# Hash-bucket attention and a MoE layer on one core: when output banks are evicted, who issues the stores, and three smaller edits

## The chip, the cores and the metric

One Trainium2 chip, one of its cores. The metric is device time in microseconds (us) of one execution. Engines: TensorE (PE, with PEld for its weight loads), VectorE (DVE), ScalarE (ACT), GpSimd (POOL) and SyncE (SP, which in this kernel issues DMAs).

## What is computed

Attention over 4 batches, 8 heads, 768 positions and 64 dimensions, where a query sees only the keys of its own hash bucket; then a two-layer feed-forward net, all to float32 accuracy.

```python
q_bits = einsum('bhsd,dk->bhsk', q, proj) > 0        # k has its own; proj is 64 x 6
mask = q_bucket[:, :, :, None] == k_bucket[:, :, None, :]
scores = where(mask, q @ k.T / 8, -1e9)
attn = softmax(scores) @ v
x = attn as [3072 tokens, 512]
h = x @ w_in                                         # 512 x 2048
g = where(h > 0, h, exp(min(h, 0)) - 1)
out = g @ w_out                                      # 2048 x 512
```

## The kernel before

Each float32 operand is scaled by a power of two and split into a float16 high half and a float16 low half; a product is then three float16 matmuls. `scaled` (L139 to L147, most of it ACT at L143) makes a high half, `rest` (L149 to L155, DVE at L152) a low half. The table `ENGINES` says which engine makes which half; its first entry holds while weights are still being decoded (`now[0]` is 0), its second after that.

The work goes in **slots**. A slot is one tile of scores: 128 queries of one head against all 768 keys (`scores`, L503): four matmuls into the one buffer of PSUM tile `s`, which DVE empties with a clamp that also takes the row maximum (`pt`, L519). Every second slot ACT takes the exponentials (L535), ACT and DVE split them into halves (`hl`), and SP transposes those by DMA (`PT`, L550). Six slots make a pair of heads for half a sequence, 24 a **chunk** (3 x 128 tokens); there are eight chunks, two to a batch. Four slots after a pair, `attend` multiplies with V (`av`, L558).

While slots of later chunks run, `moe_stream` gives PE the MoE of an earlier chunk in small pieces: for each of 16 blocks `f` of the hidden layer, `first` (12 matmuls into `h`, L584, then ACT at L595 and L598, DVE at L599, and the two halves of `g`), and two blocks later `second` (9 matmuls, L620: three for each of the chunk's three token tiles `t`). The results stay in PSUM for all 16 blocks: `banks` are two banks of one tile `o` (t = 0 and 1) and a tile `o2` (t = 2). At the last block each is evicted by `scaled("out", ...)` into one of two pieces of SBUF, `area["ot"]` (shown as `W`, for it lies in the tile of the weights), and stored to `out` (L632, by SP). ACT evicts t = 0 and 2, DVE t = 1 (L145). From slot 30 on the order on PE is the order in which the program was written (`manual_schedule`, L888); on the other engines, and before that slot, a scheduler places instructions.

In the first 40 slots or so the kernel also reads both weight matrices, which come as 64-bit numbers, decodes them to float32 (`wdecode`) and splits them (`wsplit`, 32 of them); `weights` (L833) hands this out, six steps a slot. For each batch V is loaded, its squares summed by ACT, and `scale` then takes the bound: a maximum over four sums (`vx`, DVE, L411), a matmul with ones that adds over the partitions (`sum`, PE, L184) and a few small DVE operations (`powers`); `vdue` (L774 to L779) says at which slot each of these steps is written. `behind_max` places DVE work behind the latest `pt`. K and Q of later pairs are prepared in the same way; their high halves are `n_hi`.

Of the kernel before, what the change touches and what calls it, by code (L numbers as in the profile page):

```python
# [10 lines left out]
F32 = mybir.dt.float32  # L11
I32 = mybir.dt.int32
AF = mybir.ActivationFunctionType
ALU = mybir.AluOpType
AX = mybir.AxisListType
# [32 lines left out]
ENGINES = {  # L48
    "p_hi": ("A", "A"),
    "p_lo": ("V", "V"),  # L50
    "n_hi": ("VA", "A"),
    "n_lo": ("V", "V"),
    "v_hi": ("A", "A"),
    "v_lo": ("V", "V"),
# [12 lines left out]
def lsh_attention_moe(  # L67
# [315 lines left out]
    def prep_v(b):  # L383
        st = {"f": [], "v": [None] * NP}

        def load():
            mx = small.tile([P, NP], F32, tag="vx", name="vx")
            for p in range(NP):
                f = vpool.tile([P, 2, NC, D], F32, tag="v", name="vf")
                with tc.issue_after(ks[b, V_AFTER]["done"].ins) if b == 0 else nullcontext():  # L390
                    nc.sync.dma_start(
                        f.rearrange("p h c d -> p h (c d)"),
                        v[b, 2 * p : 2 * p + 2].rearrange("h (p c) d -> p h (c d)", c=NC),
                    )
                st["f"].append(f)
            st["mx"] = mx
            if b == 0:
                for p in range(NP):
                    sums(p)

        def sums(p):
            f = st["f"][p]
            squares(st["mx"][:, p : p + 1], f.rearrange("p h c d -> p (h c d)"), steady.k1 if b else junk0)

        def scale():
            with behind_max():
                bound()

        def bound():
            m1 = small.tile([P, 1], F32, tag="vx1", name="vx1")  # L410
            nc.vector.tensor_reduce(m1, st["mx"], axis=AX.X, op=ALU.max)  # L411
            st["ex"], st["sc"] = powers(m1, 1, 2.0**-34, V_TOP, "v", squares=True)

        def split(p):
            f = st["f"][p]
            t = vpool.tile([P, 2, NC, 2, D], F16, tag="v", name="vhl")
            st["v"][p] = t
            for j in range(2):
                scaled("v_hi", t[:, j, :, 0, :], f[:, j], st["sc"])
                rest("v_lo", t[:, j, :, 1, :], f[:, j], st["sc"], t[:, j, :, 0, :])  # L420

        parts = [lambda p=p: sums(p) for p in range(NP)] if b else []
        return st, [load] + parts + [scale] + [lambda p=p: split(p) for p in range(NP)]


    wst = {}
# [142 lines left out]
        return x16  # L569


    def moe_stream(chunks):

        pend = []
        banks = []

        def first(c, f):
            w = c["nc"] * P
            h = ps_h.tile([P, 512], F32, tag="h", name="h")[:, :w]
            g, fc = f // FG, f % FG  # L580
            n = 0
            for t in range(KT):
                for wx, xx in ((0, 0), (0, 1), (1, 0)):
                    nc.tensor.matmul(  # L584
                        h,
                        WH[:, g * KT + t, wx, fc * P : (fc + 1) * P],
                        c["xs"][t][:, xx, :],
                        start=n == 0,
                        stop=n == 3 * KT - 1,
                    )  # L590
                    n += 1
                    if n < 3 * KT:
                        yield w
            e = part("e")[:, :w]
            nc.scalar.activation(e, h, AF.Exp, scale=c["ch"])  # L595

            hp = part("hp")[:, :w]
            nc.scalar.activation(hp, h, AF.Relu, scale=c["ch"])  # L598
            nc.vector.scalar_tensor_tensor(e, e, -1.0, hp, ALU.add, ALU.min)  # L599
            g16 = part("g").rearrange("p (x n) -> p x n", x=2)[:, :, :w]  # L600
            scaled("g_hi", g16[:, 0, :], e, c["sg"])
            rest("g_lo", g16[:, 1, :], e, c["sg"], g16[:, 0, :])
            pend.append((c, f, g16))
            yield w

        def second(c, f, g16):
# [11 lines left out]
            for t in range(n):  # L618
                for i, (gx, wx) in enumerate(((0, 0), (0, 1), (1, 0))):
# [4 lines left out]
                        start=f == 0 and i == 0,  # L624
                        stop=f == NF - 1 and i == 2,
                    )
                    if f == NF - 1 and i == 2:
                        rows = out[c["b"] * S : (c["b"] + 1) * S, :].rearrange("(p c) o -> p c o", c=NC)
                        ot = part("ot")
                        with tc.high_priority():  # L630
                            scaled("out", ot, o[t][:, :DO], c["os"])
                        nc.sync.dma_start(rows[:, c["c0"] + t, :], ot)  # L632
                    yield DO

        for c in chunks:
# [140 lines left out]
        vs[b] = prep_v(b)  # L776
    for b in range(1, B):
        s0 = [c for c in chunks if c["b"] < b][-1]["end"]
        vdue += [(s0 + x, s) for x, s in zip((-16, -14, -13, -12, -11, -9, -8, -2, 4, 10), vs[b][1])]  # L779


    wq = list(wsplits)
# [50 lines left out]
    def weights(n):  # L833
        nonlocal w_credit, w_at
        w_credit += n
        while w_credit >= 1:

            at = (w_at + (2 if w_at >= NSI else 1)) * SL
            users = {x[1] for x in due} | ({"v"} if len(vdue) == NP + 2 + (B - 1) * (2 * NP + 2) else set())
            if any(a < at + SL and at < z and users & u for a, z, u in guards):  # L840
                break
            if w_at not in w64 and w_at < NSI + NSO:
# [4 lines left out]
            elif w_at < NSI + NSO:  # L847
# [2 lines left out]
                load_w()  # L850
                if w_at in (NSI, NSI + NSO):
                    wscale(w_at // (NSI + NSO))
            elif wq:
                split_w()

    def turned(p, what):
        return p < 0 or what in ks[0, p]
# [94 lines left out]
```

## Time and profile before

| | |
|---|---|
| median of three runs | 966.19 us (963.73 to 966.58) |
| the profiled execution | 964.54 us, its span 962.7 us |
| PE busy | 825.0 us (86%) |
| ACT busy | 742.0 us (77%) |
| DVE busy | 705.7 us (73%) |
| POOL busy | 2.6 us |

The span goes from the first to the last instruction; the execution's own time is 1.84 us more. Busy shares are means over stages that differ: the first 175 us with the decoding of the weights, then attention and MoE together, then from about 890 us the MoE of the last chunk alone. What bounds a stage is read from its windows and waits.

### The profile page before, as it was taken

How to read it: one execution, taken by the hardware profiler on the slowest of the kernel's cores; microseconds unless marked ns; L12 is line 12 of the kernel's file. 1: busy time of each engine (PE TensorE's matmuls, PEld its weight loads, DVE VectorE, ACT ScalarE, POOL GpSimd, SP SyncE). 2: the span in 40 equal slices, each digit the busy share in tenths (PEclk: the TensorE clock that was granted, in tenths of full speed). 3: DMA queues.
4: the chain of work that ended last, by engine and by line, in shares of the span. 5: the costliest groups of instructions: out<-in, count | busy, mean ns of one | idle time of the engine just before them, and what ended most of it. 6: DMA issues, size and time to landing. Idle time of an engine off the chain costs nothing.

```text
span 962.7 us, 14525 instructions
## 1 busy us (share of the span) xinstructions
PE 825.0 (86%) x4975; PEld 422.4 (44%) x4975; DVE 705.7 (73%) x1528; ACT 742.0 (77%) x1469; POOL 2.6 (0%) x25
## 2 busy tenths in 40 slices
PE   2536555879989999889989998989989999999997
PEld 0113222434445555444545554544545454555453
DVE  6789899898877777678767686687877687665232
ACT  5667777999879787789779797698878788786443
POOL 1000000000000000000000000000000000000000
PEclk9998665999999999899999999999999999999999
DMA  9999988676886759486887666785786767656000
GB/s 284 264 201 215 223 213 179 131 151 139 158 177 151 151 107 144 97 186 120 166 188 135 127 130 122 136 165 102 143 168 126 125 116 149 100 99 99 33 1 33
DMA packets 406121, 138.46 MB, mean 144 GB/s; under 512 B 380960, under 2 KB 398880, under 8 KB 406048
## 3 DMA queue, kind: packets, MB, share of 16 engines
q1 hardware_dynamic: 405888, 137.54, 69.4%
q8 instruction: 39, 0.64, 0.3%
q14 instruction: 34, 0.28, 0.1%
q10 hardware_dynamic: 160, 0.00, 0.0%
HBM read 35.65 MB, written 6.29 MB: 44 GB/s over the span
## 4 chain that ended last, share of the span: by engine, by line
PE 55%; DVE 16%; DMA 15%; ACT 8%; issue 4%; SPq 1%; ACTq 0%; DVEq 0%
PE o L620 18%; PE h L584 18%; PE av L558 9%; PE s L507 7%; DVE pt L519 4%; DMA O<-nat1q 3%; DVE hl L152 3%; DMA K<-natk 3%; DMA PT<-hl 3%; ACT pt L535 3%; PE z L286 2%; ACT W L143 1%; DMA W<-in_moe_w_in_dram 1%; DVE U L152 1%; DVE natk L152 1%
## 5 line engine op out<-in xcount | busy, mean ns | idle before, releaser
L620 PE MATMUL o<-W,U 128*128 128x512 f16 x1152 | 283.8, 384 | 20.0 <-ACT W L143 20.0
L584 PE MATMUL h<-x,W 128*128 128x384 f16 x1536 | 284.1, 329 | 0.0
L584 PEld LDWEIGHTS <-W 128*128 128x128 f16 x1536 | 148.2, 98 | 123.8 <-issue 24.0
L519 DVE TENSOR_SCALAR_CACHE_REDUCE pt<-s 128x768 f32<-128x768 f32 x177 | 168.2, 950 | 42.8 <-PE s L507 41.6
L535 ACT ACTIVATE pt<-pt,nb,sg 128x768 f32<-128x768 f32 x192 | 195.3, 1019 | 1.8
L152 DVE SCALAR_TENSOR_TENSOR hl<-pt,r,hl 128x768 f16<-128x768 f32 x192 | 189.9, 1011 | 9.2 <-ACT hl L143 8.9
L143 ACT ACTIVATE hl<-pt,r 128x768 f16<-128x768 f32 x192 | 168.6, 926 | 32.7 <-DVE r L545 32.1
L620 PEld LDWEIGHTS <-U 128*128 128x128 f16 x1152 | 111.8, 98 | 141.6 <-issue 28.4
L507 PE MATMUL s<-K,O 128*128 128x384 f16 x708 | 152.7, 339 | 19.0 <-DVE pt L519 15.1
L558 PE MATMUL av<-PT,vhl 128*64 128x384 f16 x1152 | 114.9, 353 | 26.4 <-DMA PT<-hl 13.7
L599 DVE SCALAR_TENSOR_TENSOR U<-U 128x384 f32<-128x384 f32 x128 | 70.8, 553 | 79.5 <-ACT U L598 79.2
L507 PEld LDWEIGHTS <-O 76*128 76x128 f16 (+1 forms) x768 | 74.8, 102 | 120.5 <-issue 42.1
L595 ACT ACTIVATE U<-h,ch 128x384 f32<-128x384 f32 x128 | 73.1, 571 | 66.8 <-PE h L584 66.3
L152 DVE SCALAR_TENSOR_TENSOR U<-U,sgg 128x384 f16<-128x384 f32 x128 | 78.4, 613 | 53.8 <-ACT U L143 53.8
L558 PEld LDWEIGHTS <-vhl 128*64 128x64 f16 x1152 | 73.2, 118 | 80.4 <-issue 16.3
L143 ACT ACTIVATE U<-U,sgg 128x384 f16<-128x384 f32 x128 | 77.8, 608 | 25.5 <-DVE U L599 25.4
L598 ACT ACTIVATE U<-h,ch 128x384 f32<-128x384 f32 x128 | 72.9, 570 | 0.0
L471 PE MATMUL acc<-W,ones 128*128 128x512 bf16 x32 | 17.0, 547 | 34.8 <-DVE W L468 33.9
L535 ACT ACTIVATION_READ_ACCUMULATOR pt<-pt,nb,sg 128x1 f32 x192 | 36.3, 189 | 0.0
L291 DVE TENSOR_SCALAR zb<-z,pjt 64x384 f16<-64x384 f32 (+1 forms) x48 | 29.1, 606 | 6.9 <-PE z L286 6.9
L532 ACT ACTIVATE nb<-m,sg 128x2 f32<-128x2 f32 x96 | 27.7, 288 | 5.4 <-DVE pt L519 4.9
L286 PE MATMUL z<-O,pjz 64*32 64x384 f16 (+1 forms) x192 | 27.5, 363 | 2.4 <-DVE w0m L186 1.7
(102 smaller groups left out, 502.7 us busy)
## 6 DMA issues: line engine op xcount, KB each, us to landing
U<-in_moe_w_in_dram SPq DMA_DIRECT2D x12, 512.0 KB
vf<-in_v_dram SPq DMA_DIRECT2D x16, 384.0 KB
U<-in_moe_w_out_dram SPq DMA_DIRECT2D x12, 512.0 KB
out_dram<-W SPq DMA_DIRECT2D x24, 256.0 KB
qst<-in_q_dram SPq DMA_DIRECT2D x30, 192.0 KB
kst<-in_k_dram SPq DMA_DIRECT2D x14, 384.0 KB
PT<-hl SPq DMA_TRANSPOSE x192
W<-in_moe_w_in_dram SPq DMA_DIRECT2D x4, 512.0 KB
```

Of the source, the lines that this page charges most:

```text
L143: nc.scalar.activation(o, x, AF.Copy, scale=s)
L152: nc.vector.scalar_tensor_tensor(o, x, s, hi, ALU.mult, ALU.subtract)
L286: nc.tensor.matmul(t[u * QD : (u + 1) * QD], pj["z"][:rows, x, :], mv, start=n == 0, stop=n == len(ways) - 1)
L507: nc.tensor.matmul(s_tile[:, n, :HALF], st[o][:rows, at, :], kst[kk][:rows, j * NC + n * HC : j * NC + (n + 1) * HC, :].rearrange("p a b - ...
L519: top = nc.vector.tensor_scalar(pt.rearrange("p (n e) -> p n e", n=2), s_tile[:, :, :HALF], CLAMP, None, ALU.max, ALU.max, accum_out=duo[0 ...
L535: nc.scalar.activation(pt, pt, AF.Exp, bias=nb[:, n : n + 1], scale=st["sg"][:, 0:1], accum_out=sm[:, n : n + 1])
L558: nc.tensor.matmul(av[j * D : (j + 1) * D], vt[:, j, c, vx, :], PTs[j][:, :, px, c, :], start=n == 0, stop=n == last,)
L584: nc.tensor.matmul(h, WH[:, g * KT + t, wx, fc * P : (fc + 1) * P], c["xs"][t][:, xx, :], start=n == 0, stop=n == 3 * KT - 1,)
L595: nc.scalar.activation(e, h, AF.Exp, scale=c["ch"])
L598: nc.scalar.activation(hp, h, AF.Relu, scale=c["ch"])
L599: nc.vector.scalar_tensor_tensor(e, e, -1.0, hp, ALU.add, ALU.min)
L620: nc.tensor.matmul(o[t][:, :DO], g16[:, gx, t * P : (t + 1) * P], WH[:, NSI + 1 + f, wx, :], start=f == 0 and i == 0, stop=f == NF - 1 and ...
```

## The change

- At the last block, nothing is evicted after t = 0. After t = 1 both banks of the tile `o` are evicted, bank 0 and then bank 1; t = 2 is evicted as before.
- The stores are issued by GpSimd instead of SP.
- V's bound is two steps: `top` (the maximum) at slot -9 from the end of the batch before, `scale` (matmul and powers) at -7. The splits of V move from -8, -2, 4, 10 to -5, 1, 6, 11. For the first batch both steps stay together.
- `n_hi` is made by ACT alone while weights are decoded (before: DVE and ACT in turn).
- Once all weights are decoded, `weights` splits only those of the MoE's present and next group of four blocks.

```diff
-    "n_hi": ("VA", "A"),
+    "n_hi": ("A", "A"),
...
+        def top():
+            m1 = small.tile([P, 1], F32, tag="vx1", name="vx1")
+            with behind_max():
+                nc.vector.tensor_reduce(m1, st["mx"], axis=AX.X, op=ALU.max)
+            st["m1"] = m1
+
         def scale():
             with behind_max():
-                bound()
-
-        def bound():
-            m1 = small.tile([P, 1], F32, tag="vx1", name="vx1")
-            nc.vector.tensor_reduce(m1, st["mx"], axis=AX.X, op=ALU.max)
-            st["ex"], st["sc"] = powers(m1, 1, 2.0**-34, V_TOP, "v", squares=True)
+                st["ex"], st["sc"] = powers(st["m1"], 1, 2.0**-34, V_TOP, "v", squares=True)
...
-        return st, [load] + parts + [scale] + [lambda p=p: split(p) for p in range(NP)]
+        return st, [load] + parts + ([top, scale] if b else [lambda: (top(), scale())]) + [lambda p=p: split(p) for p in range(NP)]
...
+    moe_at = [-FG]
...
         def first(c, f):
+            moe_at[0] = max(moe_at[0], f)
...
-                    if f == NF - 1 and i == 2:
-                        rows = out[c["b"] * S : (c["b"] + 1) * S, :].rearrange("(p c) o -> p c o", c=NC)
-                        ot = part("ot")
-                        with tc.high_priority():
-                            scaled("out", ot, o[t][:, :DO], c["os"])
-                        nc.sync.dma_start(rows[:, c["c0"] + t, :], ot)
+
+                    if f == NF - 1 and i == 2 and (t > 0 or n == 1):
+                        for u in range(t + 1) if t < 2 else (2,):
+                            rows = out[c["b"] * S : (c["b"] + 1) * S, :].rearrange("(p c) o -> p c o", c=NC)
+                            ot = part("ot")
+                            with tc.high_priority():
+                                scaled("out", ot, o[u][:, :DO], c["os"])
+                            nc.gpsimd.dma_start(rows[:, c["c0"] + u, :], ot)
...
-        vdue += [(s0 + x, s) for x, s in zip((-16, -14, -13, -12, -11, -9, -8, -2, 4, 10), vs[b][1])]
+        vdue += [(s0 + x, s) for x, s in zip((-16, -14, -13, -12, -11, -9, -7, -5, 1, 6, 11), vs[b][1])]
...
-            elif wq:
+            elif wq and (wq[0] if wq[0] < NSI else (wq[0] - NSI) // FG * KT) // KT <= moe_at[0] // FG + 1:
                 split_w()
+            else:
+                break
```

Three places show how instructions stand. (Rows are `line operation out<-in shape`; the waits that the program states are in brackets; a row that repeats the one ahead of it is left out.)

PE at the end of the first chunk, before: the last matmul of t = 0, a tile of scores, then t = 1, t = 2 (`o_1559` is the tile `o2`) and the hash bits of a later K.

```order
L620 MATMUL o<-W,U 128x512
L507 MATMUL s<-K_2175,O_2181 128x384 [waits DVE_49]
L507 MATMUL s<-K_2176,O_2182 128x384
L620 LDWEIGHTS U
L620 MATMUL o<-W,U 128x512 [waits Activation_49]
L620 MATMUL o_1559<-W,U 128x512
L286 MATMUL z<-K_2496,pjz 32x384 [waits DMAHW0_49]
```

The same place in the change (lines have moved, `o_1527` is `o2`):

```order
L624 MATMUL o<-W,U 128x512
L508 MATMUL s<-K_2175,O_2181 128x384 [waits DVE_49]
L508 MATMUL s<-K_2176,O_2182 128x384
L624 LDWEIGHTS U
L624 MATMUL o_1527<-W,U 128x512
L286 MATMUL z<-K_2496,pjz 32x384 [waits DMAHW0_49]
```

The order is the same; the wait of t = 1's first matmul for ACT is gone. All eight chunk ends read so.

DVE at the bound of the third batch's V, before: the `pt` of a slot, the maximum, then `vm`, the first reader of PE's `sum`.

```order
L519 TENSOR_SCALAR pt,m<-s 128x768 [waits PE_49]
L411 TENSOR_REDUCE vx_4260<-vx 128x1
L152 SCALAR_TENSOR_TENSOR hl<-pt,r,hl 128x768 [waits DMAHW7_49,Activation_49]
L186 TENSOR_SCALAR vm<-sum 128x1 [waits PE_49]
L152 SCALAR_TENSOR_TENSOR hl<-pt,r,hl 128x768 [waits Activation_49]
```

The same place in the change:

```order
L520 TENSOR_SCALAR pt,m<-s 128x768 [waits PE_49]
L408 TENSOR_REDUCE vx_4260<-vx 128x1
L603 SCALAR_TENSOR_TENSOR U<-U 128x384 [waits Activation_49]
L152 SCALAR_TENSOR_TENSOR hl<-pt,r,hl 128x768 [waits DMAHW1_49,Activation_49]
L152 SCALAR_TENSOR_TENSOR hl<-pt,r,hl 128x768 [waits Activation_49]
L162 COPY K_4522<-K_4521 64x1536 [waits DMAHW2_49]
L520 TENSOR_SCALAR pt,m<-s 128x768 [waits DMAHW6_49,PE_49]
L569 SCALAR_TENSOR_TENSOR x_4311<-av,x_4311 128x384 [waits Activation_49]
L520 TENSOR_SCALAR pt,m<-s 128x768 [waits DVE_49,PE_49]
L152 SCALAR_TENSOR_TENSOR hl<-pt,r,hl 128x768 [waits DMAHW7_49,Activation_49]
L186 TENSOR_SCALAR vm<-sum 128x1 [waits PE_49]
```

Two tiles of scores now lie between the maximum and the reader of `sum`; on PE `sum` stands behind two more tiles of scores too.

ACT at the end of the second chunk, before: the squares of a Q (`nat1q`), the high halves `hl`, the evictions of bank 0 and of `o2` (both `W<-o`), and between them the next exponentials.

```order
L207 ACTIVATE nat1q,qx<-qst 128x384
L143 ACTIVATE hl<-pt,r 128x768 x2
L143 ACTIVATE W<-o,os 128x512
L143 ACTIVATE U<-U,sgg 128x384
L532 ACTIVATE nb<-m,sg 128x2
L535 ACTIVATE pt,sm<-pt,nb,sg 128x768 x2
L544 ACTIVATE r<-sm 128x2
L143 ACTIVATE W<-o_1559,os 128x512
```

In the change:

```order
L207 ACTIVATE nat1q,qx<-qst 128x384
L143 ACTIVATE hl<-pt,r 128x768 x2
L143 ACTIVATE U<-U,sgg 128x384
L143 ACTIVATE W<-o,os 128x512
L533 ACTIVATE nb<-m,sg 128x2
L536 ACTIVATE pt,sm<-pt,nb,sg 128x768 x2
L599 ACTIVATE U<-h,ch 128x384
L602 ACTIVATE U<-h,ch 128x384
L545 ACTIVATE r<-sm 128x2
L143 ACTIVATE W<-o_1527,os 128x512
```

One `U` has moved ahead of the first eviction, and two activations that empty an `h` ahead of the second.

## Rows read from the trace of the kernel before

**Rows 1.** Page, part 2: TensorE's granted clock, tenths, 40 equal slices.
```profile
PEclk9998665999999999899999999999999999999999
```
**Rows 2.** Windows: start:end in us, then busy time (and count) by engine, clock, DMA.
```profile
0.00:175.00 175.00, 89.31 (x404) 37.89 (x404) 150.05 (x369) 120.67 (x233) 2.57 (x25) 0.82 0.91 224
175.00:290.00 115.00, 100.89 (x629) 51.80 (x628) 96.19 (x207) 102.59 (x205) 0.00 (x0) 0.96 0.75 152
290.00:900.00 610.00, 577.18 (x3641) 302.98 (x3640) 442.28 (x925) 493.58 (x987) 0.00 (x0) 0.98 0.69 132
```
**Rows 3.** Waits, whole span: who waited for whom: us in total, times, longest.
```profile
PE o L620 <- ACT W L143: 20.0, 8, 5.2
...
PE s L507 <- DVE pt L519: 15.1, 20, 2.5
...
PE sum L184 <- DVE vx L411: 9.2, 3, 3.9
...
ACT W L143 <- DMA out_dram<-W: 8.3, 3, 3.4
```
**Rows 4.** Windows, PE only, of the half-clock stretches around waits before `o`.
```profile
387.75:394.58 6.83, 5.01 (x16) 0.50 0.69 142
...
sum 20.48, PE 17.50; mean PE 4.38
```
**Rows 5.** Windows, PE only, of the half-clock stretches around waits before `sum`.
```profile
428.70:432.11 3.41, 3.41 (x15) 0.50 1.13 311
...
sum 13.65, PE 12.69; mean PE 4.23
```
**Rows 6.** Timeline, end of the second chunk: start, length, engine, line, tiles, [idle before].
```profile
383.52 0.81 PE L507 MATMUL s<-K,O 128*128 128x384 f16 x4
...
385.24 0.52 ACT L207 ACTIVATE nat1q<-qst 128x384 bf16<-128x384 f32 x1 [2.72 <-DMA O<-nat1q]
...
388.84 0.68 ACT L143 ACTIVATE W<-o,os 128x512 f32<-128x512 f32 x1
...
389.57 2.72 PE L620 MATMUL o<-W,U 128*128 128x512 f16 x6 [5.24 <-ACT W L143]
...
392.41 0.20 ACT L544 ACTIVATE r<-sm 128x2 f32<-128x2 f32 x1
...
395.36 0.69 ACT L143 ACTIVATE W<-o,os 128x512 f32<-128x512 f32 x1 [2.75 <-DMA out_dram<-W]
...
399.18 2.75 PE L620 MATMUL o<-W,U 128*128 128x512 f16 x12
```
**Rows 7.** Timeline, the bound of the third batch's V.
```profile
427.38 0.95 DVE L519 TENSOR_SCALAR_CACHE_REDUCE pt<-s 128x768 f32<-128x768 f32 x1
...
428.26 0.15 DVE L411 TENSOR_REDUCE vx<-vx 128x1 f32<-128x4 f32 x1
428.33 1.01 DVE L152 SCALAR_TENSOR_TENSOR hl<-pt,r,hl 128x768 f16<-128x768 f32 x1
428.46 0.16 PE L184 MATMUL sum<-vx,ones 128*128 128x1 bf16 x1 [2.67 <-DVE vx L411]
```
**Rows 8.** Timeline, the end of the program.
```profile
956.16 0.69 ACT L143 ACTIVATE W<-o,os 128x512 f32<-128x512 f32 x1 [2.18 <-PE o L620]
...
956.87 3.15 SPq L632 DMA_DIRECT2D out_dram<-W  x3
956.90 1.46 PE L620 MATMUL o<-W,U 128*128 128x512 f16 x6 [0.78 <-ACT W L143]
...
958.98 0.69 ACT L143 ACTIVATE W<-o,os 128x512 f32<-128x512 f32 x1 [2.13 <-DMA out_dram<-W]
```
**Rows 9.** Tile `natk`: duration ns least/median/most, first and last start, shape.
```profile
L143 ACT ACTIVATE natk<-kst,ks x12: 919/924/941, 202.9 to 689.1; 128x768 f16<-128x768 f32 x12
L145 DVE TENSOR_SCALAR natk<-kst,ks x2: 602/606/610, 11.2 to 80.6; 128x768 f16<-128x768 f32 x2
```

More of the change, by code (lines that the diff above doesn't have):

```diff
@@ L838, in weights @@
             at = (w_at + (2 if w_at >= NSI else 1)) * SL
-            users = {x[1] for x in due} | ({"v"} if len(vdue) == NP + 2 + (B - 1) * (2 * NP + 2) else set())
+            users = {x[1] for x in due} | ({"v"} if len(vdue) == NP + 2 + (B - 1) * (2 * NP + 3) else set())
             if any(a < at + SL and at < z and users & u for a, z, u in guards):
```

## The prediction

> **What bounds the kernel now.** I read the clock slices first, then the windows by stage, then the waits, and last the timeline at the longest waits. The slices show the granted clock of TensorE falling below full speed mainly in one early stretch [rows 1]. The windows say why there are two programs in one [rows 2]: up to 175 us PE is busy for 89.3 us of 175 and DVE for 150.1, so decoding and DVE's queue set the pace; from 290 to 900 us PE is busy for 577.2 us of 610, ACT for 493.6 and DVE for 442.3. There PE is the bound, and what counts is each microsecond in which it waits. Between the two, from 175 to 290 us, ACT (102.6 of 115) and PE (100.9) are about equally loaded.
>
> In the waits of the whole span [rows 3], PE loses 20.0 us in 8 waits before `o` that an ACT eviction (`W L143`) ends: one for each chunk. It loses 9.2 us in 3 waits before `sum`, ended by DVE's maximum over V: one for each batch after the first. Around these waits the clock is at 1.2 instead of 2.4 GHz in seven stretches: four around waits before `o`, three around waits before `sum`; no other stretch after 175 us is that slow but the last 3.6 us. PE was busy for 17.50 us in the four and 12.69 us in the three [rows 4, 5]; at the half clock half of that work time is lost, 8.75 and 6.35 us.
>
> The timeline shows the mechanism at the second chunk's end [rows 6]. PE ends a tile of scores at 384.33 and cannot write t = 1 into bank 1 until ACT has read bank 0 of the same tile, though these are different banks. ACT had itself waited 2.72 us for a transpose that still read `nat1q`, and the eviction stands behind other work at 388.84. PE resumes at 389.57, at half clock. At V's bound [rows 7] DVE is late with a `pt`, the maximum follows it at once, and PE stands at the matmul that needs it.
>
> **The change, part by part.** The sum is made against the profiled execution, 964.5 us; the median of the three runs is 1.65 us above it, and 0.3% (2.9 us) is about what a measurement of this kernel can tell from no change.
>
> *Evictions.* Removed: the wait before t = 1 at all eight ends, as the first order shows. At most that gives 20.0 + 8.75 = 28.75 us. Not all of it stays, since ACT's own work is no shorter. I follow the second end [rows 6] with the third order. From 388.84 ACT runs an eviction, one `U`, `nb`, two `pt` and `r` until 392.61; the change has the same plus two short activations ahead of `o2`'s eviction, which I estimate to end some 2 us later, at about 394.5, if the store of bank 0 has landed by then (before, ACT stood 2.75 us for it). PE needs that eviction for the next chunk's third tile. Before, it came there at about 400.5: the `o` row that starts at 399.18 holds twelve matmuls in 2.75 us, and six of them go ahead. So about 6 of the 7.7 us lost at this place (5.24 of wait and half of 5.01 us) can come back: 78%. Where no transpose held ACT the wait is some 2 us and ACT is busier, so the share is lower. I take 70% for all: 20.1 us. Late next are `o2`'s eviction and DVE's `pt`. The new order also lets the first `o` of the next chunk wait for both banks; two `first` groups stand ahead of it on PE, so it costs nothing unless ACT is more than these behind. Ends of the range: 45% and 100%, 12.9 and 28.75 us.
>
> *V's bound.* The maximum keeps its place behind the same `pt`; the matmul moves two slots later on PE (second order). PE can't reach it before DVE has done a `pt` that stands behind the maximum, so the wait is gone, at most 9.2 + 6.35 = 15.6 us. Behind DVE's `pt` PE may wait a little more at the next scores, and the first of the three lies where ACT is 89% busy. I take 70%: 10.9 us, ends 45% and 100% (7.0 and 15.6). V's splits come 1 to 3 slots later; the first stands 14 slots ahead of the `av` that needs it, the last 16, so they cost nothing.
>
> *`n_hi`.* Four tiles of K go from DVE to ACT (two are named `natk`, two lie in `W`). DVE loses 4 x 0.606 = 2.4 us, ACT gains 4 x 0.924 = 3.7 us [rows 9]. DVE has 25 us of idle time before 175 us, ACT 54 [rows 2], so I give DVE's saving a bit under half: 1 us. But the scheduler has also rearranged the start: V's splits and one decoding come ahead of the first `hl`. Such a move can cost a wait for a weight's load or save one; bounds from nothing in the change but from the idle time: 8 us either way, a third of DVE's 25.
>
> *Weights.* The limit costs nothing: on ACT the 32 splits stand behind the 12th to the 40th `hl` before and behind the 10th to the 38th now, with the same instructions, since the scheduler moves ready ones ahead anyway.
>
> *Stores.* The 24 issues leave SP's queue, where a store could hold back transposes behind it; GpSimd has nothing else to do by then. At the end of the program [rows 8] PE's wait of 0.78 us goes, but bank 0 is evicted only after t = 1, three matmuls later, at about 956.8, and its store starts at 957.5 instead of 956.87. It landed 2.1 us after its issue and released ACT at 958.98, so now at 959.6 at the earliest; the last store ended the span 3.0 us after ACT's end at 959.67. With the same landing the end is 0.6 us later than before; where a landing kept ACT waiting for 3.4 us [rows 3], it would be some 1.9. A GpSimd store is not in the trace: I take 1.0 us, nearest to the row at the end, and 0.6 to 3 as ends. The Trainium skill's page "DMA: Bandwidth & Descriptors" (section "Specifications") gives about 1 us to the first byte on GpSimd's path against 0.6 on SP's; by it the end would be 0.4 later and the sum 933.9, and no run here shows it yet.
>
> Sum: 964.5 - 20.1 - 10.9 - 1.0 + 1.0 = 933.5 us; the runs' median lies above the profiled execution, so I say 934.
>
> **The rivals.**
>
> *ACT becomes the bound at the chunk ends.* Then a removed wait comes back before `h` or `o2`, and part of the half clock with it. For it: between 290 and 900 us ACT is busy for 81%, and it was fully busy behind each eviction. Against it: PE is busy for 95% there. With 45% of both terms: 964.5 - 12.9 - 7.0 = 944.6, and 945 to 953 with the start's bad end.
>
> *GpSimd's stores wait for DVE.* ACT's eviction of t = 2 needs the piece of SBUF that bank 0's store reads. The stretch that covers it is 3.1 us (from 389.52 to 392.61 in rows 6) or more; a landing was 2.1 us in rows 8. If a store's issue is held behind two long DVE instructions of 1.01 us each [rows 7], it lands after 4.1 us and costs 1 us at eight ends: 942. The Trainium skill's page "SBUF — State Buffer" (section "SBUF: two separate sides") has the mechanism: DVE and GpSimd share a port pair, a DVE instruction in a two-port mode locks GpSimd out of writing a store's descriptors, and it advises issue from ACT or SP. This speaks against the change; the trace of before has no such store.
>
> *Slower.* The same place, worse: each microsecond of landing beyond 3.1 stalls ACT at eight ends. The 31 us gained are gone at 31 / 8 = 3.9 us beyond the cover, a landing of 7.0 us. With 8.5 us: 8 x 5.4 = 43 us, 964.5 - 31 + 43 = 977. That is four times the shortest row.
>
> *The start decides.* The scheduler's new order of the first 175 us costs more than 8 us, say 25 (all of DVE's idle time once more): 958.
>
> *It doesn't do what it says.* The wait before t = 1 would have to remain; the order shows it gone, so it could only move as a whole to the next `s` or `h`: 964.
>
> **How the numbers follow.** Forecast case 0.66; ACT as bound 0.16; stores behind DVE 0.08; the start 0.04; no change 0.03; slower 0.03. The low end: both waits fully back, and a start that is 2 us better: 964.5 - 28.75 - 15.6 - 2 + 1 = 919. The high end takes the ACT case with the start's bad end: 953. Beyond these lie some 2 in 10. Faster by over 0.3%: 0.66 + 0.16 + 0.08 + most of the start's 0.04, less a little for a bad sum: 0.91; within: 0.04; slower: 0.05.
>
> **What would show it.** In the changed profile: no wait of PE before `o` for `W L143` above 1 us at t = 1, and what is left at the first `o` or `o2` of the next chunk; no wait of `sum` for `vx`; none of the seven half-clock stretches at these places; PE busier than 95% from 290 to 900 us; PE's first MoE matmuls within 8 us of where they were; ACT's waits for a store below 1 us at the seven inner ends. Wrong would be: as many microseconds of PE waiting before `h`, `s` or `av` as are gone before `o` and `sum`; ACT waiting for stores by more than 3 us at each end; or a stage before 175 us that has grown by more than 8 us.

## The result, and the profile after

The changed kernel takes 953.92 us (median of 4 runs, 953.06 to 955.42) against 965.97 us before: a ratio of 0.9871 [0.9851, 0.9890], 12 us faster. The forecast was 934 us with a range of 919 to 953: the direction was right, the gain was 12 us where 32 were forecast, and the time lies 0.9 us above the range. The profiled execution took 954.10 us, its span 952.0 us.

First the slices and the windows of the changed kernel, with the columns of [rows 1, 2].

```profile
PEclk9998656999999999999999999999999999999998
```
```profile
0.00:175.00 175.00, 88.05 (x398) 35.45 (x399) 150.42 (x369) 125.18 (x243) 2.57 (x25) 0.81 0.93 225
175.00:290.00 115.00, 103.36 (x651) 53.32 (x649) 95.44 (x202) 100.30 (x200) 0.00 (x0) 0.97 0.76 148
290.00:900.00 610.00, 582.21 (x3699) 309.24 (x3697) 443.86 (x932) 497.07 (x1000) 11.52 (x21) 1.00 0.71 133
```

From 290 to 900 us the granted clock is full on average (1.00), and PE is busy for 95.4% instead of 94.6%. The waits of the whole span answer to [rows 3]:

```profile
PE s L508 <- DVE pt L520: 31.7, 31, 4.5
PE av L559 <- DMA PT<-hl: 16.7, 11, 3.2
...
PE o L624 <- ACT W L143: 4.2, 4, 2.0
...
PE sum L184 <- DVE x L569: 1.4, 1, 1.4
```
```profile
ACT W L143 <- DMA out_dram<-W: 9.0, 6, 3.0
```

At the places that the change aimed at both waits are gone: before `o` 20.0 us have become 4.2, now elsewhere, and none of the 9.2 us before `sum` is put down to the maximum any more. But PE waits 31.7 us before `s` where it waited 15.1, and 16.7 before `av`, where the same view of the kernel before has this:

```profile
PE av L558 <- DMA PT<-hl: 13.7, 5, 6.8
```

To see where the time went I cut both traces at the first MoE matmul (the first `h`) and at the last matmul into `o`, and summed PE's idle time between the cuts:

| | before | after | difference |
|---|---|---|---|
| start to the first `h` | 169.2 | 169.9 | +0.7 |
| first `h` to the last `o` | 788.8 | 773.5 | -15.3 |
| of it PE idle | 48.5 | 40.3 | -8.2 |
| of it PE busy | 740.3 | 733.2 | -7.1 |
| time between these cuts at the half clock (1.2 GHz) | 34.1 | 10.2 | -23.9 |
| last `o` to the end of the span | 4.7 | 8.6 | +3.9 |

So the stretch that was to give 31 us gave 15.3, and the end took 3.9 of them back. These are single executions. Two later kernels, in which PE, ACT and DVE run the same instructions in the same order as in the change (the third place for the last eviction, below), show how well they repeat: 772.9 and 773.5 us between the cuts, 37.6 and 38.5 us of it idle, 17.1 and 13.7 us at the half clock, the first `h` at 170.9 and 172.2 us. So a length between the cuts repeats within some 0.6 us in these three, its split into idle and busy time is loose by some 3 us, and the first `h` by some 2. Of the single chunks the first, second and fifth became 2.9 to 4.9 us shorter, the last two 1.3 and 0.9; the third, fourth and sixth stayed within 1.0 us of where they were.

The second chunk's end shows a place that went as forecast in the main [rows 6]:

```profile
388.57 0.67 ACT L143 ACTIVATE W<-o,os 128x512 f32<-128x512 f32 x1
...
392.42 0.20 ACT L545 ACTIVATE r<-sm 128x2 f32<-128x2 f32 x1
393.71 0.69 ACT L143 ACTIVATE W<-o,os 128x512 f32<-128x512 f32 x1 [1.10 <-DMA out_dram<-W]
```
```profile
387.53 0.81 PE L508 MATMUL s<-K,O 128*128 128x384 f16 x4 [0.51 <-DVE pt L520]
388.18 2.76 PE L588 MATMUL h<-x,W 128*128 128x384 f16 x16
391.97 0.81 PE L508 MATMUL s<-K,O 128*128 128x384 f16 x4 [1.03 <-DVE pt L520]
392.62 1.46 PE L624 MATMUL o<-W,U 128*128 128x512 f16 x6
394.45 1.46 PE L624 MATMUL o<-W,U 128*128 128x512 f16 x6 [0.37 <-ACT W L143]
```

The 5.24 us before `o` are 0.37, and 1.54 us before `s` stand in their place; the chunk is 4.9 us shorter. At the bound of the third batch's V [rows 7] the maximum again follows its `pt` at 423.15 us, and nobody waits for it. But around and behind that `pt` PE stops three times in 30 us, before `av`, before `s` and before the next `av`:

```profile
422.99 3.08 PE L559 MATMUL av<-PT,vhl 128*64 128x384 f16 x35 [0.74 <-DMA PT<-hl]
...
430.17 0.81 PE L508 MATMUL s<-K,O 128*128 128x384 f16 x4 [0.74 <-DVE pt L520]
...
432.12 0.17 PE L184 MATMUL sum<-vx,ones 128*128 128x1 bf16 x1
```
```profile
447.89 0.35 PE L559 MATMUL av<-PT,vhl 128*64 128x384 f16 x1
451.40 4.79 PE L559 MATMUL av<-PT,vhl 128*64 128x384 f16 x35 [3.16 <-DMA PT<-hl]
```

These are 4.6 us. Before, the same stretch had the 2.67 us before `sum` and 1.96 us before a later `av`, 4.6 us too. Around the bound of the second batch's V, where PE had stood 3.87 us before `sum`, the two longest waits before `s` of the changed kernel stand, 2.58 us up to 236.70 us and this one:

```profile
205.98 1.46 PE L508 MATMUL s<-K,O 128*128 128x384 f16 x4 [4.51 <-DVE pt L520]
```

While V is split, ACT has no idle time at all (18.00 of 18 us, the fourth busy time):

```profile
436.00:454.00 18.00, 14.84 (x92) 7.19 (x91) 15.38 (x29) 18.00 (x38) 0.00 (x0) 0.93 0.64 106
```

The end of the program [rows 8]:

```profile
943.19 0.69 ACT L143 ACTIVATE W<-o,os 128x512 f32<-128x512 f32 x1 [2.83 <-PE o L624]
943.91 0.75 DVE L145 TENSOR_SCALAR W<-o,os 128x512 f32<-128x512 f32 x1 [2.89 <-ACT W L143]
944.17 0.54 POOL L638 DMA_DIRECT2D out_dram<-W  x1 [54.23 <-ACT W L143]
944.95 0.54 POOL L638 DMA_DIRECT2D out_dram<-W  x1 [0.25 <-DVE W L145]
946.86 0.69 ACT L143 ACTIVATE W<-o,os 128x512 f32<-128x512 f32 x1 [2.99 <-DMA out_dram<-W]
947.84 0.54 POOL L638 DMA_DIRECT2D out_dram<-W  x1 [2.35 <-ACT W L143]
```

The last matmul into `o` starts at 943.42 us. The last eviction starts 3.4 us behind it (before: 1.0), and the span ends 4.4 us after that eviction's end (before: 3.0).

### The profile page after: what moved, and what is told of

It reads as the page before. It is cut to its first block, busy times and chain, and to the rows that moved or that the text cites. A ratio compares the mean times of both kernels' runs of the same rounds, so it can differ in the third digit from the quotient of the medians.

```text
span 952.0 us, 14531 instructions
## 1 busy us (share of the span) xinstructions
PE 817.4 (86%) x4975; PEld 420.6 (44%) x4975; DVE 703.4 (74%) x1524; ACT 741.4 (78%) x1473; POOL 15.7 (2%) x49
## 4 chain that ended last, share of the span: by engine, by line
issue 77%; PE 11%; DMA 5%; DVE 3%; ACT 2%; POOL 1%; POOLq 0%; ACTq 0%; DVEq 0%
PE o L624 3%; PE h L588 3%; PE av L559 2%; PE s L508 2%; DMA K<-natk 1%; DMA O<-nat1q 1%; DMA out_dram<-W 1%; POOL out_dram L638 1%; ACT pt L536 1%; DVE pt L520 1%; DVE hl L152 1%; DMA PT<-hl 1%; DMA vf<-in_v_dram 0%; DVE natk L152 0%; ACT hl L143 0%
## 5 line engine op out<-in xcount | busy, mean ns | idle before, releaser
L624 PE MATMUL o<-W,U 128*128 128x512 f16 x1152 | 280.3, 379 | 4.3 <-ACT W L143 4.2
L588 PE MATMUL h<-x,W 128*128 128x384 f16 x1536 | 280.8, 327 | 0.8 <-ACT x L568 0.6
L508 PE MATMUL s<-K,O 128*128 128x384 f16 x708 | 153.8, 341 | 32.1 <-DVE pt L520 31.7
L624 PEld LDWEIGHTS <-U 128*128 128x128 f16 x1152 | 111.0, 98 | 125.4 <-issue 11.7
L559 PE MATMUL av<-PT,vhl 128*64 128x384 f16 x1152 | 113.8, 347 | 27.1 <-DMA PT<-hl 16.7
L508 PEld LDWEIGHTS <-O 128*128 128x128 f16 (+1 forms) x768 | 74.9, 102 | 129.9 <-issue 55.0
L472 PE MATMUL acc<-W,ones 128*128 128x512 bf16 x32 | 17.1, 554 | 33.9 <-DVE W L469 33.9
L207 ACT ACTIVATE nat1q<-qst 128x384 bf16<-128x384 f32 x30 | 15.5, 517 | 18.9 <-DMA O<-nat1q 18.1
```

Of the source, the lines that this page charges most:

```text
L508: nc.tensor.matmul(s_tile[:, n, :HALF], st[o][:rows, at, :], kst[kk][:rows, j * NC + n * HC : j * NC + (n + 1) * HC, :].rearrange("p a b - ...
L559: nc.tensor.matmul(av[j * D : (j + 1) * D], vt[:, j, c, vx, :], PTs[j][:, :, px, c, :], start=n == 0, stop=n == last,)
L588: nc.tensor.matmul(h, WH[:, g * KT + t, wx, fc * P : (fc + 1) * P], c["xs"][t][:, xx, :], start=n == 0, stop=n == 3 * KT - 1,)
L624: nc.tensor.matmul(o[t][:, :DO], g16[:, gx, t * P : (t + 1) * P], WH[:, NSI + 1 + f, wx, :], start=f == 0 and i == 0, stop=f == NF - 1 and ...
```

## The experiments

Theory A was that a removed wait mostly comes back before `s` and `av`; rivals were GpSimd's stores (B), the later places of V's splits (C) and the start (D). Times are medians, ratios are to the kernel before; a difference of ratios is told in us of 965. "Between the cuts" is the stretch from the first `h` to the last `o` in one profiled execution.

**One part undone at a time.** The stores by SP again:

```diff
-                            nc.gpsimd.dma_start(rows[:, c["c0"] + u, :], ot)
+                            nc.sync.dma_start(rows[:, c["c0"] + u, :], ot)
```

> The changed kernel with its 24 output stores issued by SP again. Theory A (the removed waits came back before s and av, where DVE's pt and the transposes of PT are late, and GpSimd's stores cost only at the end of the program): only the tail of 8.6 us from the last o to the span's end shrinks, by 3 to 4 us, so 950 to 951 us; PE's waits before s ended by pt stay at 25 to 32 us. Theory B (stores that land 4 to 6.6 us after their issue hold up ACT, and through ACT the pt of DVE and PE): 946 us or less, ACT's waits for out_dram fall from 9.0 us to about 3, and PE's waits before s to about 20 us. If stores in SP's queue hold back the transposes of PT: 955 us or more, with more waiting before av.

Measured: 955.84 us, 0.9901 [0.9864, 0.9938]. The tail shrank from 8.6 to 6.3 us and ACT's waits for stores to 3.9 us, so B's first half holds; but B's gain did not come. None of the three cases came whole: A's time is missed by some 5 us, and the waits before `av`, which stores in SP's queue were to lengthen, fell from 9.1 to 7.6 us between the cuts. With SP's stores the scheduler puts `o2`'s eviction behind `hl`, and PE waits 14.2 us before `o` instead of 4.2. At the second chunk's end of this kernel:

```profile
394.88 1.76 ACT L143 ACTIVATE hl<-pt,r 128x768 f16<-128x768 f32 x2
396.53 0.68 ACT L143 ACTIVATE W<-o,os 128x512 f32<-128x512 f32 x1
```
```profile
397.26 1.45 PE L624 MATMUL o<-W,U 128*128 128x512 f16 x6 [2.25 <-ACT W L143]
```

Ten microseconds more of this wait made the stretch from the first `h` to the last `o` only 2.1 us longer: a first sign of what such waits are worth. What the stores alone cost in mid-run stays open here, since the order moved with them.

Each bank evicted at its own time:

```diff
-                    if f == NF - 1 and i == 2 and (t > 0 or n == 1):
-                        for u in range(t + 1) if t < 2 else (2,):
+                    if f == NF - 1 and i == 2:
+                        for u in (t,):
```

> The changed kernel with each bank evicted as soon as it is complete, as before the change; the rest of the change stays. The prediction's step would give 20.1 us of loss, 974 us. Theory A (two fifths or less of a removed wait is kept, since the same ACT and DVE work then ends a wait before s): about 9 us slower than the changed kernel, 961 to 965 us, with some 20 us of PE waiting before o for W and about 8 us less before s and av. If the evictions brought nothing at all and the whole gain is the V bound's: 953 to 956 us.

Measured: 968.49 us, 1.0032 [1.0014, 1.0050]: 14.6 us slower than the change by the medians, 15.5 by the ratios, more than A had put and less than the prediction's 20.1. It is also 3.1 ± 1.7 us slower than the kernel before, so the rest of the change brought nothing by itself; chunk by chunk its trace agrees with that of the kernel before within 1.4 us. Its waits:

```profile
PE s L508 <- DVE pt L520: 25.2, 23, 4.0
PE o L624 <- ACT W L143: 21.4, 8, 5.2
PE av L559 <- DMA PT<-hl: 15.8, 9, 3.4
```

Of the 17.2 us that go before `o`, 6.5 come back before `s` and 0.9 before `av` (3.0 and 1.3 if the change is read from the first of the two later traces of its order, with 28.2 and 17.1 us). Between the cuts the difference is 13.1 us; this trace is of the fastest of ten executions, 3.6 us below their median, so 13.1 is more likely low than high.

V's bound in one step, with the old slots for its splits:

```diff
-([top, scale] if b else [lambda: (top(), scale())])
+[lambda: (top(), scale())]
...
-(-16, -14, -13, -12, -11, -9, -7, -5, 1, 6, 11)
+(-16, -14, -13, -12, -11, -9, -8, -2, 4, 10)
...
```

> The changed kernel with V's bound in one step and V's splits at their old places. The prediction's step would give 10.9 us of loss, 965 us. Theory A: 3 to 6 us slower, 957 to 960 us, with 9 us of PE waiting before sum for the maximum and 3 to 5 us less before s and av. Theory C (V's splits at their later places make pt and the transposes late in the chunks that hold them, as the third chunk gained nothing): 954 us or less, and the third chunk not longer than with the change.

Measured: 956.19 us, 0.9900 [0.9868, 0.9931], by the ratios 2.8 ± 3.6 us slower than the change; between the cuts 2.2 us longer. The waits before `sum` are back (7.6 us), and those before `av` for `PT` are 3.9 us shorter. PE is idle for 40.1 us between the cuts, as in the change (37.6 to 40.3 in its three traces): the wait before `sum` stands in the place of others. The two undoings together (13.1 and 2.2 us between the cuts) are just the 15.3 us of the change, by one trace of each.

The start as it was:

```diff
-    "n_hi": ("A", "A"),
+    "n_hi": ("VA", "A"),
...
-            elif wq and (wq[0] if wq[0] < NSI else (wq[0] - NSI) // FG * KT) // KT <= moe_at[0] // FG + 1:
+            elif wq:
...
-            else:
-                break
```

> The changed kernel with K's splits in turns on DVE and ACT again and no limit on the weights' splits, which gives back the old order of the first 200 us. Theory A: within 2 us of the changed kernel, 952 to 956 us, with the first MoE matmul at 169 to 170 us in both. Theory D (the weights' splits, now among the slots from 200 us on, cost PE the waits of 4.51 us at 205.98 and 2.58 us at 236.70): 947 to 950 us, and these two waits gone.

Measured: 954.38 us, 0.9889 [0.9850, 0.9928], 1.7 ± 4.2 us slower than the change by the ratios, the first `h` at 170.3 us. Of D's two waits the one of 4.51 us is gone, as D said; the other is 3.50 us instead of 2.58, and those before `av` are 2.5 us longer between the cuts. The gain of 4 to 7 us that D wanted did not come, so D falls: this wait too was exchanged for others.

**Where V's splits stand.**

```diff
-(-16, -14, -13, -12, -11, -9, -7, -5, 1, 6, 11)
+(-16, -14, -13, -12, -11, -9, -7, -6, -2, 4, 10)
```

> The changed kernel (V's bound in two steps) with V's four splits at slots -6, -2, 4 and 10 of a batch, about where they stood before the change, in place of -5, 1, 6 and 11. PE's order is the same in both. Theory C (the later splits put vhl work of ACT and DVE ahead of the hl that the transposes of PT wait for): the 9.1 us of PE waiting before av for PT between the first MoE matmul and the last o fall to about 3, and the time by 5 to 6 us, to 948 to 949 us. Theory A (any wait that is removed there comes back, wherever the splits stand): 953 to 955 us, with the waits before s and av together (33.8 us) unchanged within 2 us.

Measured: 955.40 us, 0.9879 [0.9833, 0.9925], with more waiting before `av` between the cuts (11.7 us), not less. And the bound in one step with the late splits:

```diff
-([top, scale] if b else [lambda: (top(), scale())])
+[lambda: (top(), scale())]
...
-(-16, -14, -13, -12, -11, -9, -7, -5, 1, 6, 11)
+(-16, -14, -13, -12, -11, -9, -5, 1, 6, 11)
...
```

> The changed kernel with V's bound in one step at slot -9, as before the change, but V's splits at the change's later slots -5, 1, 6 and 11. It parts the two halves of that edit. Theory C: the waits before sum (some 8 us) are back and those before av for PT stay at 8 to 9 us, so it is slower than the run with the bound in one step and the old slots (956.2 us): 960 to 963 us. Theory A: within 2 us of that run, 954 to 958 us.

Measured: 953.57 us, 0.9868 [0.9826, 0.9910]. Its waits:

```profile
PE s L508 <- DVE pt L520: 31.4, 30, 3.8
PE av L559 <- DMA PT<-hl: 11.5, 8, 2.4
...
PE sum L184 <- DVE vx L408: 7.6, 3, 2.7
```

C falls twice. This kernel has 7.6 us of waiting before `sum` that the change does not have, and is as fast. By the medians, the ratios and the cuts the bound in two steps is worth between 0 and 3 us, with intervals that reach 6 to 7.

**The end of the program.** A third place for the last eviction:

```diff
-                            ot = part("ot")
+                            ot = W[:, 1, :] if u == 2 and c is chunks[-1] else part("ot")
```

> The changed kernel with another place in SBUF (a piece of the input weights that nothing reads any more) for the last tile of the last chunk, so that its eviction waits for no store; the order of every engine is the same, and the stores stay on GpSimd. If the tail grew because ACT waits 2.99 us there for a GpSimd store to land, the tail from the last o to the span's end falls from 8.6 to about 6.2 us and the time to 951.5 us. If the end is set by something else behind the last store: 8 us or more remain and 954 us.

Measured: 953.10 us, 0.9860 [0.9819, 0.9901], the tail 6.8 us. And with the last chunk's three stores by SP:

```diff
-nc.gpsimd.dma_start(
+(nc.sync if c is chunks[-1] else nc.gpsimd).dma_start(
```

> As the run before it, and the last chunk's three stores are issued by SP instead of GpSimd; the other 21 stay on GpSimd, and no engine's arithmetic moves. With the end 3.0 us after the last issue, as SP's last store showed before the change, against 4.2 us: the tail falls to about 5 us and the time to 950 to 950.5 us. If GpSimd's issue costs nothing over SP's: the same as the run before it.

Measured: 950.15 us, 0.9830 [0.9783, 0.9876], the tail 5.7 us, 1.1 us shorter than with GpSimd. The times differ by 3.0 us, but the intervals overlap; only the tail's 2.9 us, from 8.6 to 5.7, is read from the traces.

**Less work on ACT.** If ACT's full queue around V's splits is what brings the waits back, taking work off it must help, and the two steps must then be worth something.

```diff
-    "v_hi": ("A", "A"),
+    "v_hi": ("A", "P"),
```

> The changed kernel with the upper halves of V's splits for batches 1 to 3 made by GpSimd, which is idle there, in place of ACT: 24 instructions of 0.55 us (13 us, 4.4 us a batch) leave ACT; PE's order is the same. Theory A in its sharper form (around V's bound ACT's queue is full, so whatever wait of PE is removed there, PE waits for ACT's hl, or for DVE behind it, a little later): the waits before s and av between the first MoE matmul and the last o fall from 33.8 us by 6 us or more, and the time to 944 to 949 us. If ACT's load is not what makes PE wait there: 952 to 956 us. If DVE waits long for a GpSimd instruction: 958 us or more, and the trace shows that wait in front of vhl on DVE.

Measured: 947.93 us, 0.9818 [0.9779, 0.9858], 6.9 us less between the cuts. There the waits before `av` for `PT` are 3.4 us instead of 9.1; those before `s` are as long as in the change (25.1 and 24.7 us). On top of it V's bound in one step with the old slots, by the same diff as above:

> The run before it with V's bound in one step and the old slots, as before the change. Theory A: with room on ACT the removed wait before sum no longer comes back, so the bound in two steps is worth something here: this run is 4 us or more slower than the one before it (with ACT as it is, the two-step bound was worth 0 to 2 us). If the waits come back for another reason: within 2 us of the run before it.

Measured: 949.51 us, 0.9838 [0.9796, 0.9879], between the cuts 0.2 us longer than the run before it, by the ratios 1.9 ± 5.5 us slower. And the two steps with DVE in place of GpSimd:

```diff
-    "v_hi": ("A", "A"),
+    "v_hi": ("A", "V"),
```

> The changed kernel with the upper halves of V's splits for batches 1 to 3 made by DVE in place of ACT. If ACT alone is the bound around V's bound: 948 to 951 us. If DVE is as full there, or PE waits for DVE's pt through it: 954 us or more, with more waiting before s.

Measured: 946.47 us, 0.9805 [0.9765, 0.9845]. So ACT's load does hold PE up there: moving 24 instructions of some 0.6 us gave 6.0 and 7.5 us by the medians (5.1 ± 4.2 and 6.4 ± 4.3 by the ratios). But with ACT relieved, one step is as good as two within the noise. So ACT's load looks like a cost of its own, and not like the reason why the removed wait came back.

**What PE's time is worth.** The last theory, G: PE goes through these places and meets ACT and DVE later, so a wait of PE there is mostly not on the path that sets the end. Then work put there must cost little. Its rival H: the time counts in full there, and the gain went into the other order that the scheduler gave ACT and DVE. Here the work is put at V's bound, 16 matmuls at each of three places and 32 in the run after it:

```diff
...
+            for _ in range(16 * extra.pop() if extra else 0):
+                nc.tensor.matmul(h, WH[:, g * KT, 0, fc * P : (fc + 1) * P], c["xs"][0][:, 0, :], start=True, stop=True)
             for t in range(KT):
...
             vdue.pop(0)[1]()
+            if len(vdue) in [(2 * NP + 3) * k + NP + 1 for k in range(B - 1)]:
+                extra.append(1)
```

> The changed kernel with 16 matmuls more (128x384, 0.163 us each, 2.6 us, their result overwritten at once) on PE at the places where the wait for V's bound stood, three times: 7.8 us of PE time in the place of the wait that the change removed. Theory G (PE's time there is worth little, since PE, once through, meets ACT and DVE later anyway): 954 to 957 us. Theory H (PE's time there counts in full, and the gain was lost to the other order that the scheduler gave ACT and DVE): 960 to 962 us.

> The changed kernel with 32 instead of 16 matmuls more (128x384, 0.163 us each) on PE at each of the three places where the wait for V's bound stood: 15.6 us of PE time. The run with 16 was 1.0 us slower than the changed kernel by the medians, 3.7 us by the ratios to the kernel before, of 7.8 us. If PE's time there is worth an eighth of its length: 956 us. If it is worth a half: 961 to 962 us. If what exceeds the removed wait counts in full (2.6 us of each 5.2 us lie in the place of the wait of 2.7 us that stood there, the rest beyond it): 962 to 964 us. If all counts: 969 us.

In the next two the count is `16 if f == 2 and c is not chunks[0] else 0`, and then `16 if f == NF // 2 and c in (chunks[1], chunks[3], chunks[5], chunks[6]) else 0`.

> The same 16 matmuls at the ends of chunks 1 to 7, in the third group of the next chunk, just ahead of the last output group: 7 times 2.6 = 18.2 us of PE time. Theory G with the price that undoing the evictions showed (14.6 of the 28.75 us of wait and half clock, one half): 961 to 965 us. If PE's time counts in full there: 970 to 972 us.

> The same 16 matmuls in the middle of the second, fourth, sixth and seventh chunks, where PE ran without waits before the change: 4 times 2.6 = 10.4 us of PE time. Here PE is the bound by the prediction's reading (busy for 95% of the time), so all of it counts: 963 to 965 us. If PE's time is worth as little there as at V's bound: 954 to 958 us.

Measured, against the changed kernel (us; the last column is the difference of the two ratios times 965, with the root of the sum of the squares of their half intervals):

| PE work added | idle between the cuts | length between the cuts | median | by the ratios |
|---|---|---|---|---|
| 7.8 at V's bound | -5.0 | +1.2 | +1.0 | +3.7 ± 3.6 |
| 15.6 at V's bound | -9.1 | +6.0 | +6.1 | +5.6 ± 3.1 |
| 18.2 at chunk ends | -9.2 | +8.8 | +8.1 | +9.6 ± 2.5 |
| 10.4 in mid-chunk | -2.5 | +7.8 | +9.8 | +12.5 ± 2.7 |

A microsecond of PE is worth most or all of itself in mid-chunk, about half at the chunk ends and an eighth to a half at V's bound (the medians and cuts give the lower figures there, the ratios the higher). So H, which had put 960 to 962 us for the first row and all of 15.6 for the second, falls; between V's bound and the chunk ends the intervals show no difference. The rest is taken out of waits elsewhere, as far as the idle time can tell, which is loose by some 3 us. With the 15.6 us added:

```profile
PE s L508 <- DVE pt L520: 22.6, 24, 3.9
PE av L559 <- DMA PT<-hl: 14.8, 10, 2.4
```

Without any change of their own, the waits before `s` fall from 31.7 us (28.2 and 30.9 in the two later traces of the change's order) to 22.6: it is the same slack, taken at another place. At the last two chunk ends, where no scores are left, the 2.6 us count in full (87.2 to 89.9 and 58.4 to 61.0 us a chunk); the other five ends took some 3.4 of their 13.0 us. One caution: with more matmuls the scheduler gives ACT and DVE another order, and a single chunk came out up to 6 us longer or 4 us shorter without having any added work; the totals carry the table, no single chunk does.

**A faster version.** DVE makes V's upper halves, the last eviction has its own place, and the last three stores go by SP, by the diffs above:

> The changed kernel with V's upper halves made by DVE for batches 1 to 3, another place for the last chunk's third output tile and its stores on SP. The two gains lie in different places and add up: 946.5 - 3.8 = 942.7 us, 941 to 945 us. If the tail's gain is lost on the way: 946 us.

Measured: 944.56 us (943.63 to 946.67), 0.9793 [0.9776, 0.9809], 9 us faster than the change and within what was expected. Its end:

```profile
936.15 1.33 ACT L143 ACTIVATE W<-o,os 128x512 f32<-128x512 f32 x2 [2.83 <-PE o L624]
936.86 1.49 SPq L638 DMA_DIRECT2D out_dram<-W  x3
936.87 0.75 DVE L145 TENSOR_SCALAR W<-o,os 128x512 f32<-128x512 f32 x1 [2.90 <-ACT W L143]
```

The two evictions of ACT follow each other, and the tail is 5.7 us.

## Why the prediction was wrong in size

- **V's bound**, forecast 10.9 us, measured 0 to 3 (2.2 between the cuts). This is the step that failed most: "Behind DVE's `pt` PE may wait a little more at the next scores ... I take 70%". The wait before `sum` did go, as the order had shown, but PE's idle time did not go with it: with the bound in one step PE is idle for 40.1 us between the cuts, with two for 37.6 to 40.3. The row that ended the wait (the maximum) stood right behind a late `pt` [rows 7]; as I read it, what PE waited for was DVE's pace, and the maximum only gave it its name. PE met the next late `pt` at `s` and the transposes at `av`. Work put in its place costs an eighth to a half of itself, so the 9.2 us of wait had to be priced at some 1 to 4 us, not at 70%. Nor is the half clock safe ground for a price: the forecast counted 6.35 us of it here, while three traces of one order of PE, ACT and DVE have 10.2, 17.1 and 13.7 us at the half clock at the same length within 0.6 us.
- **Evictions**, forecast 20.1 us, measured 14.6 by the medians (15.5 ± 2.5 by the ratios, 13.1 between the cuts). The mechanism was right: the wait before t = 1 is gone at all ends, and what is left stands at the next chunk's `o` and `o2`, 2.0 us at most. Mis-sized was the share: it was worked out at the second end, the longest wait of the eight, where 78% could come back by its working (4.9 of 7.7 us, 64%, did), and 70% was taken for all. With the evictions alone undone the first, second and fifth chunks are 3.4 to 4.2 us longer, the third, fourth and sixth within half a microsecond of the change. By the medians half of the 28.75 us came, which is also what the added work at these ends was worth.
- **The start** (`n_hi`, the weights), forecast a gain of 1.0 with 8 us either way: the first `h` came 0.7 us later, less than the 2.3 us by which it moves between traces of one order, and undoing these edits gave nothing. Within its bounds, and it decided nothing. The wait of 4.51 us at 205.98 us goes with the start's edits, but its removal is worth nothing that can be told.
- **The tail**, forecast 1.0 with 0.6 to 3 as ends, measured 3.9. Bank 0's eviction now starts 0.2 us before the last `o` instead of 1.8: 1.6 us. Its store was issued 0.3 us after the eviction instead of at once and released ACT 2.7 us after its issue instead of 2.1: 0.9 us. The span ends 4.4 us after the last eviction instead of 3.0: 1.4 us. The forecast's 0.6 was against the old time line; the 0.78 us of PE's wait that goes there was already in the 20.0 us of the evictions, so behind the last `o` its own rows give 1.4. The delays of issue and the longer end were left out.
- **ACT's waits for stores** were to be below 1 us at the inner ends; they were 6.0 us at five (9.0 less the 3.0 at the end), so the cover of 3.1 us was short by about 1 us each.
- **The rivals.** "ACT becomes the bound" came nearest: the waits do come back, and some half of the first term and a fifth or less of the second is kept, but they come back before `s` and `av`, not before `h` or `o2`, and with ACT relieved V's bound was worth no more; 45% of that term was still too high. GpSimd's stores held ACT up for 9.0 us, hardly more than SP's did before (8.3 us, [rows 3]); the slower case needed 43. Of the signs named for a wrong forecast one came true by two thirds: of 25.0 us gone before `o` and `sum`, 12.6 came back before `s` and 4.0 before `av` between the cuts. The other two, long waits for stores at each end and a longer start, did not.

Between the cuts the miss adds up: 7.0 us on the evictions, 8.7 on the bound, 1.7 on the start and 2.9 on the tail are 20.3 of the 20.6 us between the sum of 933.5 and the profiled 954.1. That it closes so well is in part luck: each term is read from single executions, and the start's lies within its own spread.

What stays open is which part of DVE's and ACT's order sets the pace that PE meets; with V's splits moved, with ACT's load lowered and with the start undone, one wait was still exchanged for another.

## What to carry to other kernels

A wait in the profile tells where PE stood, not what its removal is worth: a few redundant matmuls, put where a removed wait had stood, measure it. Here the price that they gave, half at the chunk ends and an eighth to a half at V's bound, is of the size of what the removals gave; they were run in the changed kernel, so that they give the price beforehand is not shown. Where the releaser of a wait stands right behind another late instruction on its engine, price the wait by that instruction. And look for work to take off the engine that is full there: 24 short instructions moved from ACT to DVE gave more by the medians than the reordering of V's bound (7.5 against some 2 us).

## What the hardware showed

- A store of 256 KB by GpSimd released ACT 2.7 us after its issue at the quiet end (944.17 to 946.86 us) and 4.2 us after it in mid-run (389.53, the first row below, to 393.71 us). SP's store before the change took up to 5.8 us at that place, from the eviction's end to ACT's restart [rows 6] (4.5 us with GpSimd, counted in the same way), though 2.1 at the end [rows 8].

```profile
389.53 0.54 POOL L638 DMA_DIRECT2D out_dram<-W  x1 [92.70 <-ACT nb L533]
391.34 0.54 POOL L638 DMA_DIRECT2D out_dram<-W  x1 [1.27 <-DVE W L145]
```

  The Trainium skill's page "DMA: Bandwidth & Descriptors" (section "Anatomy of one DMA — SWDGE (gpsimd) path") fits such a transfer as 2.0 us and its bytes by 436 GB/s: 2.6 us, an estimate with which the quiet landing agrees and the one in mid-run does not. The Trainium skill's page "SBUF — State Buffer" (section "SBUF: two separate sides"), weighed in the prediction, would have DVE hold such stores up; 4.2 against 2.7 us goes that way, but SP's 5.8 us there does not need it, and no run here tells them apart.
- Three stores issued close together ended the span later than spaced ones: with SP, 3.8 us after the end of the last issue (938.35 to 942.1 us above) against 2.7 before the change (960.02 to 962.7 us). Two more runs agree: 3.75 us with the last chunk's three stores close together, 2.68 us with all stores by SP and spaced.
- GpSimd was no slower than ACT at V's upper halves by the median (one instruction took 1.39 us), and DVE a third faster. Rows of the tile `vhl` (least, median and most ns), of the run with GpSimd and of the run with DVE:

```profile
L147 POOL TENSOR_SCALAR vhl<-vf,vs x24: 576/589/1392, 231.8 to 652.2; 128x384 f16<-128x384 f32 x24
L143 ACT ACTIVATE vhl<-vf,vs x8: 597/598/602, 46.8 to 52.9; 128x384 f16<-128x384 f32 x8
```
```profile
L145 DVE TENSOR_SCALAR vhl<-vf,vs x24: 389/412/421, 231.4 to 654.0; 128x384 f16<-128x384 f32 x24
```
